# Two attention layers in one kernel: the linear layer's token forms prepared during the other layer, with another order of pairs

## The chip, the cores and the metric

The kernel runs on one core of a Trainium2 chip. TensorE (PE) multiplies matrices into eight accumulation banks. VectorE (DVE), ScalarE (ACT) and GpSimd (POOL) do the rest; POOL does not touch the banks here. SyncE (SP) issues all transfers from one queue, in order. The metric is the device time of one execution, in microseconds; less is better. The kernel before took 1781.55 us (median of three runs, 1781.36 to 1782.36).

## The reference

Two independent layers of 2048 tokens, width 1024 and 32 heads of 32 are computed and put side by side:

```python
# layer A: four segments of 512 tokens, causal softmax inside a segment,
# and a memory (M, z) that is read before and added to after each one
p = softmax(qs @ ks.T * scale + mask);  a_dot = p @ vs
a_mem = (phi(qs) @ M) / (phi(qs) @ z + 1e-6)
o = g * a_mem + (1 - g) * a_dot
M = M + phi(ks).T @ vs;  z = z + phi(ks).sum()

# layer B: linear attention with a learned feature map per head
q, k, v = split(x @ wqkv)
phi_q = concat(softmax(q @ w_phi), softmax(-q @ w_phi))     # and phi_k likewise
kv = phi_k.T @ v;  z = phi_k.sum()                          # over all 2048 tokens
o = (phi_q @ kv) / (phi_q @ z + 1e-6)
```

Each layer ends with a product by its output weights `wo`. Layer A is called attention here, layer B the linear layer.

## The kernel before, in words

**Precision.** Every large product is made of three 16-bit products. An fp32 operand is scaled, its upper half is copied to fp16 by ACT, and the rest is subtracted into a second fp16 half by DVE (`halves`, L388) or by POOL (`forms`, L466). The scale comes from the largest absolute value: a reduction per partition on DVE, a tiny product with a column of ones on PE that spreads it, and a few small operations on DVE.

**Strassen forms.** The linear layer works on pairs of 128-token blocks, eight pairs in all. A product of a pair (256 tokens by 1024) with a weight block is done as seven smaller products of combinations of blocks ("forms") in place of eight (`strassen`, L549 for the products, L555 and L559 for the sums of results on ACT and DVE). The seven forms of a pair take 7 x 256 KB. `xpair` makes them: it loads the raw tokens, finds the scale (L490 to L504), forms four sums on POOL (L458), splits the seven forms into halves (L388 or L466), and stores them in a scratch tensor `xf_d` (L526). `xkept` (L536) loads forms that were stored before, in two or three large transfers. The seven forms of a weight matrix are 1 MB each (`load_forms`, L475).

**Stages.** (1) Attention, up to about 930 us: 32 units, each a group of four heads in one segment; segments 0 and 1 first, then 2 and 3. Beside it the linear layer's query and key weights are multiplied with the feature map and turned into forms (`fold`). Segment 2 is loaded and split at unit 3 and segment 3 at unit 7 (`load_seg`), both needed only from unit 16 on. In the tail, pairs 6 and 7 get their forms, their values are computed and put away in `v_d`. (2) The key stage, to about 1265: for pairs 0 to 7 in this order a key product, the exponentials (L1112 to L1125), for pairs 0 to 5 the value product (splits at L1150 and L1152), and the sums kv (L1266). The next pair's forms are made meanwhile. `keep_bo` splits the linear layer's output weights here. (3) The query stage, to about 1600: queries, numerators, output product. (4) Attention's output product.

**What sets the order.** Every operation is recorded with an engine, a duration, a priority and its dependences, and a planner (`Graph.run`) writes the order of each engine from these: of the operations that are ready it takes the one with the lowest priority number. On the chip each engine then works through its list in that order and waits where an operand is late. `PB = 100` lies above all priorities of attention, so key-stage work fills attention's gaps. Buffers named `S0` to `S15` are slots of 8 KB per partition that pass from one stage to the next; a new owner waits for the readers of the one before.

Of the kernel before, what the change touches and what calls it, by code (L numbers as in the profile page):

```python
# [18 lines left out]
S = 2048  # L19
# [10 lines left out]
XS = (("S8", 4), ("S12", 3))  # L30
# [4 lines left out]
XL = (5, -0.2)  # L35
# [3 lines left out]
KS = (10, 14, 13, 4, 5, 6, 7)  # L39
XPLAN = ((None, 0, 0), (None, 1, 1), ((2, 3, "add"), 4, 3), ((0, 2, "subtract"), 2, 4), ((4, 0, "subtract"), 0, 2),  # L40
         ((1, 0, "subtract"), 1, 5), (None, 3, 6))
WPLAN = ((None, 0, 0), (None, 2, 1), (None, 3, 5), ((1, 0, "subtract"), 0, 3), ((3, 1, "subtract"), 1, 4),
# [201 lines left out]
def tile_kernel(ctx: ExitStack, tc: tile.TileContext, ax, aw, awv, awo, beta, bx, bwqk, bwv, bphi, bwo, out):  # L244
# [41 lines left out]
    wm = const.tile([128, 2], F32, name="wm")  # L286
    nc.gpsimd.memset(wm, 1.0)
# [8 lines left out]
    big = const.tile([128, 2], F32, name="big")  # L296
# [5 lines left out]
    bdm = ca.tile([128, NG, 132], F32, name="bdm")  # L302
# [181 lines left out]

    def xpair(p, raws, slots, prio, kind="pv", mode=DVE):
# [3 lines left out]
        for i, (rb, rv) in enumerate(raws):  # L489
# [4 lines left out]
        op(DVE, 0.1, lambda: nc.vector.tensor_reduce(top()[:, 0:1], top(), axis=AX.X, op=OP.max), w=[top], prio=prio)  # L494
        ps = bank(kind, [128, 2], "xscale")
        op(PE, 0.14, lambda: nc.tensor.matmul(ps(), top()[:, 0:1].to_broadcast([128, 128]), wm, start=True, stop=True),
           r=[top, wmb], w=[ps], prio=prio, short=True)
        op(DVE, 0.1, lambda: nc.vector.tensor_scalar(pst[:, p, 0:2], ps(), 2.0 ** -13, 1e-24, op0=OP.mult, op1=OP.max),
           r=[ps], w=[(pstb, (p, 0))], prio=prio)
        op(DVE, 0.12, lambda: nc.vector.reciprocal(pst[:, p, 2:4], pst[:, p, 0:2]), r=[(pstb, (p, 0))], w=[(pstb, (p, 1))], prio=prio)  # L500
        op(DVE, 0.1, lambda: nc.vector.scalar_tensor_tensor(
# [27 lines left out]
        return view_  # L529

    def xkept(p, slots, prio):

        t, view_, _ = xforms(slots)
        i = 0
# [1038 lines left out]
```

## Time and profile before

| | |
|---|---|
| median of three runs | 1781.55 us |
| profiled execution: first to last instruction | 1779.5 us |
| PE busy | 1715.4 us (96%) |
| DVE busy | 1457.1 us (82%) |
| ACT busy | 1130.8 us (64%) |
| POOL busy | 922.3 us (52%) |
| DMA, share of 16 engines | 44.9% |
| mean granted PE clock | 0.992 |

The busy time of PE counts overlapping products once. A wait is put down to the instruction that ended last before it; where an instruction waits for several, it can have been another. In a row of a group stand line, engine, operation, the names of the result and the operands, sizes and count, then busy us and mean ns of one, then the idle time just before. The names of the lines in the rows are those of the kernel before.

### The profile page before, as it was taken

How to read it: one execution, taken by the hardware profiler on the slowest of the kernel's cores; microseconds unless marked ns; L12 is line 12 of the kernel's file. 1: busy time of each engine (PE TensorE's matmuls, PEld its weight loads, DVE VectorE, ACT ScalarE, POOL GpSimd, SP SyncE). 2: the span in 40 equal slices, each digit the busy share in tenths (PEclk: the TensorE clock that was granted, in tenths of full speed). 3: DMA queues.
4: the chain of work that ended last, by engine and by line, in shares of the span. 5: the costliest groups of instructions: out<-in, count | busy, mean ns of one | idle time of the engine just before them, and what ended most of it. 6: DMA issues, size and time to landing. Idle time of an engine off the chain costs nothing. (4 is left out here: it accounts for less than half of the span.)

```text
span 1779.5 us, 38925 instructions
## 1 busy us (share of the span) xinstructions
PE 1715.4 (96%) x14712; PEld 1040.4 (58%) x14712; DVE 1457.1 (82%) x3367; ACT 1130.8 (64%) x2095; POOL 922.3 (52%) x1141
## 2 busy tenths in 40 slices
PE   7999999999999999999989989999899999999999
PEld 5767766677776777677644444444555444554444
DVE  6989989899787888788877999988997888877541
ACT  6897886987866878689674756444644454344441
POOL 6445454555756687777583544433456677431000
PEclk9999999999999999999989999999999999999999
DMA  6546555574545453674565244276411333133311
GB/s 208 169 144 183 159 153 158 167 225 129 160 128 156 109 179 110 161 217 121 179 202 193 96 168 137 113 272 227 139 49 63 119 125 107 66 143 137 119 65 65
DMA packets 173260, 258.92 MB, mean 146 GB/s; under 512 B 69904, under 2 KB 122896, under 8 KB 164368
## 3 DMA queue, kind: packets, MB, share of 16 engines
q1 hardware_dynamic: 173072, 256.44, 44.9%
q8 instruction: 115, 1.88, 0.4%
q14 instruction: 73, 0.60, 0.1%
HBM read 145.44 MB, written 85.00 MB: 129 GB/s over the span
## 5 line engine op out<-in xcount | busy, mean ns | idle before, releaser
L359 PE MATMUL proj<-S,S 128*128 128x128 f16 (+1 forms) x3072 | 502.7, 299 | 5.5 <-ACT S L386 3.6
L359 PEld LDWEIGHTS <-S 128*128 128x128 f16 x4608 | 331.3, 99 | 153.6 <-issue 8.9
L549 PE MATMUL proj<-S,S 128*128 128x512 f16 x1488 | 348.7, 382 | 12.3 <-ACT cs L555 3.9
L549 PEld LDWEIGHTS <-S 128*128 128x128 f16 x1968 | 189.0, 99 | 231.3 <-issue 17.2
L880 POOL TENSOR_SCALAR_AFFINE_SELECT ph<-ph 128x256 f16<-128x256 f16 (+1 forms) x448 | 196.3, 460 | 171.8 <-DVE ph L874 134.9
L874 DVE SCALAR_TENSOR_TENSOR ph<-s,ph 128x512 f16<-128x512 f32 x320 | 210.4, 683 | 56.5 <-ACT ph L873 54.5
L775 DVE CUSTOM_DVE_ANT_0 s<-s,causal 128x512 f32<-128x512 f32 (+3 forms) x512 | 242.3, 510 | 12.0 <-PE s L769 8.4
L871 ACT ACTIVATE s<-s,bd 128x512 f32<-128x512 f32 x320 | 212.2, 710 | 21.8 <-PE s L867 21.4
L873 ACT ACTIVATE ph<-s 128x512 f16<-128x512 f32 x320 | 190.4, 656 | 0.6
L1119 ACT ACTIVATE e<-e,sk 128x256 f32<-128x256 f32 x256 | 113.9, 497 | 98.3 <-DVE e L1116 94.5
L359 PE MATMUL misc<-S,ot 128*128 128x512 f16 x768 | 174.1, 379 | 0.0
L1415 POOL TENSOR_TENSOR e<-e,zb 128x512 f32<-128x512 f32 x64 | 84.5, 1343 | 71.5 <-DVE r L1122 65.8
L359 PEld LDWEIGHTS <-ot 128*128 128x128 f16 x768 | 73.4, 98 | 82.1
L769 PE MATMUL s<-S 96*128 96x512 f16 (+3 forms) x512 | 113.3, 300 | 5.8 <-DVE mt L775 4.2
L867 PE MATMUL s<-S 104*128 104x512 f16 (+3 forms) x512 | 113.9, 300 | 1.5 <-DVE quad L1011 0.8
L359 PE MATMUL proj<-wv,S 128*128 128x128 f16 x1536 | 104.2, 221 | 0.3 <-DVE mt L775 0.3
L903 PEld LDWEIGHTS <-ph 128*128 128x128 f16 x2560 | 87.8, 96 | 18.0 <-POOL ph L880 2.0
L1226 POOL TENSOR_TENSOR e<-e,r 128x1024 f32<-128x1024 f32 x32 | 64.4, 2017 | 61.3 <-DVE r L1125 50.4
L903 PE MATMUL pv<-vl,ph 128*128 128x66 f16 (+1 forms) x2560 | 92.9, 185 | 2.2 <-POOL ph L880 1.6
L1122 DVE TENSOR_REDUCE r<-e 128x32 f32<-128x1024 f32 x64 | 76.7, 1205 | 21.6 <-ACT e L1119 21.6
L1428 POOL TENSOR_TENSOR e<-e,r 128x1024 f32<-128x1024 f32 x32 | 62.9, 1970 | 41.9 <-DVE r L1426 38.3
L549 PE MATMUL s<-S,S 128*128 128x512 f16 x324 | 77.1, 379 | 1.8 <-ACT cs L555 1.8
(302 smaller groups left out, 3334.8 us busy)
## 6 DMA issues: line engine op xcount, KB each, us to landing
S<-h SPq DMA_DIRECT2D x192, 128.0 KB
S<-wf_d SPq DMA_DIRECT2D x21, 1024.0 KB
st<-bwqk SPq DMA_DIRECT2D x64, 256.0 KB
wf_d<-fo SPq DMA_DIRECT2D x48, 256.0 KB
out<-os SPq DMA_DIRECT2D x40, 256.0 KB
wf_d<-oT SPq DMA_DIRECT2D x36, 256.0 KB
S<-xf_d SPq DMA_DIRECT2D x9, 1024.0 KB
S<-aw SPq DMA_DIRECT2D x16, 512.0 KB
```

Source lines behind the costliest of these rows:

```text
L359: op(PE, dur, lambda c=c, a=a, b=b, lv=lv, rv=rv: nc.tensor.matmul(pv(), lv(), rv(), start=(c == 0 and a + b == 0), stop=(c == n - 1 and a ...
L549: op(PE, 0.215, lambda n=n, a=a, b=b, lv=lv, rv=rv: nc.tensor.matmul(ps(), lv(), rv(), start=(start and n == 0 and a + b == 0), stop=(n == ...
L769: nc.tensor.matmul(ps()[:, o:o + 128 * i + 128], st()[0:96, 0, h, 128 * i:128 * i + 128], st()[0:96, 1, h, 0:128 * i + 128], start=True, s ...
L775: dve(0.12 + 0.00113 * n, lambda h=h, i=i, o=o, n=n: nc.vector.tensor_tensor_reduce(ps()[:, o:o + n], ps()[:, o:o + n], causal[:, 512 - n: ...
L867: nc.tensor.matmul(ps()[:, o:o + n], st()[0:104, 1, h, 128 * j:128 * j + 128], st()[0:104, 0, h, 128 * j:512], start=True, stop=True)
L871: act(0.59, lambda: nc.scalar.activation(ps(), ps(), AF.Exp, bias=0.0, scale=bd()[:, 4, i2, 0:1]), r=[(bd, i2)], w=[ps])
L873: act(0.5, lambda: nc.scalar.activation(ph()[:, 0], ps(), AF.Copy, scale=2.0 ** 14), r=[ps], w=[(ph, 0)])
L874: dve(0.6, lambda: nc.vector.scalar_tensor_tensor(ph()[:, 1], ps(), 2.0 ** 14, ph()[:, 0], op0=OP.mult, op1=OP.subtract), r=[ps, (ph, 0)], ...
L880: nc.gpsimd.affine_select(pd, pd, pattern=[[0, n], [1, 128]], compare_op=OP.is_ge, fill=0.0, base=0, channel_multiplier=-1)
L903: nc.tensor.matmul(ps()[:, i, n0:n1], ph()[:, a, o:o + 128], vl()[:, j, h, n0:n1], start=(i == 0 and a == 0), stop=(j == min(i, 2)), skip_ ...
L1119: op(ACT, 0.41, lambda i=i: nc.scalar.activation(e()[:, 4 * i:4 * i + 4], e()[:, 4 * i:4 * i + 4], AF.Exp, bias=0.0, scale=sk()[:, i:i + 1 ...
L1415: op(POOL, 1.35, lambda a=a, h0=h0, e=e: nc.gpsimd.tensor_tensor(e()[:, 8 * a:8 * a + 8], e()[:, 8 * a:8 * a + 8], zv()[:, h0:h0 + 8], op= ...
```

## The change

1. **Preparation in attention.** A new function `prepare` makes the forms of pairs 6, 7, 0, 1 and 2 beside units 4, 6, 8, 15 and 27 of attention, in slots that are free there. DVE does the two maxima, ACT scales the raw blocks and makes the upper halves, POOL makes the four sums and all seven lower halves. Each form goes to `xf_d` by its own transfer. Pairs 3, 4 and 5 are prepared by the same function at the first three steps of the key stage, in `zb` and `kls`.
2. **Segments 2 and 3** are loaded at units 10 and 11 in place of 3 and 7, since the slots they use hold raw tokens first.
3. **Scales.** Token scales (`token_scale`) are found per pair, those of the values (`value_scales`) together, at unit 28 for five pairs.
4. **Tail.** The values of pairs 6, 7 and 0 are computed there, from forms that are loaded; pair 0's stay in the two `h3` buffers.
5. **Key stage.** The order of pairs is 0, 1, 6, 2, 3, 4, 7, 5; the last pair's values come before its keys. All pairs share one pair of buffers, and `xkept` reloads each of the seven forms alone as soon as its last reader is done. `keep_bo` is moved to steps 3 and 4 and its splits go to ACT and POOL. The seven query weight forms are loaded at the last step, where before six of them were loaded from the seventh step on.
6. **Query stage.** The second pair's forms have buffers of their own; the reloads are single there too.
7. Smaller: the masked memory update is two DVE operations with a small mask; halves of the value weights pass through new buffers `fp` and `fq`; other slots for the key weights.

```diff
-XS = (("S8", 4), ("S12", 3))
+XS = (("S10", 4), ("S14", 3))
+XB = (("S8", 4), ("S12", 3))
+SEQ = (0, 1, 6, 2, 3, 4, 7, 5)
+VFIRST = (7,)
+WQAT = 7
-KS = (10, 14, 13, 4, 5, 6, 7)
+KS = (8, 12, 13, 4, 5, 6, 7)
+PREP = {4: (6, 4), 6: (7, 5), 8: (0, 6), 15: (1, 11), 27: (2, 11)}
+SEGS = {10: 2, 11: 3}
+LATE = {0: 3, 1: 4, 2: 5}
+KEEPBO = {3: 0, 4: 1}
...
     def xkept(p, slots, prio):
-        t, view_, _ = xforms(slots)
-        i = 0
-        for b, (_, n) in zip(t, slots):
-            op(SP, 0.6, lambda b=b, i=i, n=n: nc.sync.dma_start(b(), xf_d[p, :, i:i + n]),
...
+        if slots is not XS:
+            t, view_, where = xforms(slots)
+        else:
+            t, view_, where = resident.get(0) or resident.setdefault(0, xforms(slots))
+        for f in XORDER:
+            b, i = where[f]
+            op(SP, 0.6, lambda b=b, i=i, f=f: nc.sync.dma_start(b()[:, i], xf_d[p, :, f]),
+               r=[(xfb, (p, f))], w=[(b, (f, a)) for a in range(2)], prio=prio, lat=1.0, kb=256)
         return view_
...
+    def prepare(p, prio, slot=None, dep=()):
+        late = slot is None
+        t = G.buf("b", [128, 2, 2, 512], F32, "zb") if late else G.buf("slot", [128, 2, 2, 512], F32, f"S{slot}")
+        top = G.buf("stage", [128, 2], F32, "xt", 2)
+        for i in range(2):
+            op(SP, 0.6, lambda i=i: nc.sync.dma_start(t()[:, i].rearrange("p a b -> p (a b)"), bx[2 * p + i].rearrange("p c n -> p (c n)")),
+               r=dep, w=[(t, (i, 0)), (t, (i, 1))], prio=prio, lat=1.0, kb=512)
+            op(DVE, 1.2, lambda i=i: nc.vector.tensor_reduce(
+                top()[:, i:i + 1], t()[:, i], axis=AX.XY, op=OP.max, apply_absolute_value=True),
...
+        token_scale(p, top, prio, "misc")
+        for i in range(2):
+            op(ACT, 1.05, lambda i=i: nc.scalar.activation(t()[:, i], t()[:, i], AF.Copy, scale=pst[:, p, 3:4]),
...
+        for n, (comb, k, f) in enumerate(XSELF):
...
+                op(POOL, 1.28, lambda i=i, j=j, k=k, o=o: nc.gpsimd.tensor_tensor(v(k), v(i), v(j), op=o),
...
+            op(ACT, 0.53, lambda h=h, k=k: nc.scalar.activation(h()[:, 0], v(k), AF.Copy), r=[key], w=[hk[0]], prio=prio)
+            e, ns, d = (DVE, nc.vector, 0.7) if n in LOWV else (POOL, nc.gpsimd, 1.28)
+            op(e, d, lambda h=h, k=k, ns=ns: ns.tensor_tensor(h()[:, 1], v(k), h()[:, 0], op=OP.subtract),
...
-        if u in (3, 7):
-            load_seg(2 + u // 4, 2 * u + 2.5, DVE)
+        if u in SEGS:
+            load_seg(SEGS[u], 2 * u + 2.5, DVE)
...
+        if u in PREP:
+            prepare(PREP[u][0], 2 * u + 4.5, PREP[u][1], [(un[u]["h3"], (1, 1))])
...
-    for n, p in enumerate(VT):
-        raw = G.buf("a", [128, 2, NC, 128], F32, "wv", 1)
...
+    for n, p in enumerate(VT + (0,)):
+        x = xkept(p, XB if n == 1 else XS, L - XL[n])
...
-    for p in range(NT // 2):
-        P = PB + 2 * p
-        if p in (1, 2):
-            keep_bo(p - 1, P + 0.5)
+    for at_, p in enumerate(SEQ):
+        P = PB + 2 * at_
+        if at_ in LATE:
+            prepare(LATE[at_], P + 0.5)
+            value_scales(LATE[at_], 1, LATE[at_], P + 0.5, "pv")
+        if at_ in KEEPBO:
+            keep_bo(KEEPBO[at_], P + 0.5)
...
+        if at_ in VFIRST:
+            strassen(x, wvf, P - 0.3, KB, CS, vout(p, vs, P - 0.3))
+            strassen(x, wkf, P, KB, CS, kout)
+        if at_ == WQAT:
+            wqf = load_forms(0, VS, P + 0.1, [])
+        if at_ < 7:
+            xn = xkept(SEQ[at_ + 1], XS, P - 0.5)
```

The order that results, at three places. First DVE in unit 8 of attention, before; `s,mt` are the row maxima of the scores, which the unit's later products wait for, and `xsc` marks the split of an input segment:

```order
L775 ISA s,mt<-s,causal 128x128
L775 ISA mt 128x1
L775 ISA s,mt<-s,causal 128x256
L775 ISA mt 128x1
L388 SCALAR_TENSOR_TENSOR S_4783<-S_4668,xsc,S_4783 128x512 x4
L775 ISA s,mt<-s,causal 128x256
L775 ISA mt 128x1
L775 ISA s,mt<-s,causal 128x512
```

The same four splits (second half of segment 3) now, in unit 13; L961 is the division of a finished unit:

```order
L807 ISA s,mt<-s,causal 128x128
L807 ISA mt 128x1
L807 ISA s,mt<-s,causal 128x512
L807 ISA mt 128x1
L961 TENSOR_TENSOR osum<-oall,rd 128x4x4x32
L398 SCALAR_TENSOR_TENSOR S_7266<-S_7166,xsc,S_7266 128x512 x4
L822 SCALAR_TENSOR_TENSOR mh<-mh,mt 128x4x4
```

The burst moved five units on and is still four long. Second, DVE in the key stage before; `mx`, `e` and `r` belong to the exponentials, `kls<-zb` are output weights and `S<-h` the next pair's forms:

```order
L1116 TENSOR_TENSOR e<-mx,cs 128x16x32
L388 SCALAR_TENSOR_TENSOR kls<-zb,wsc,kls 128x512 x4
L1114 TENSOR_TENSOR e<-cs,mx 128x16x32
L1116 TENSOR_TENSOR e<-mx,cs 128x16x32
L1112 TENSOR_REDUCE mx<-proj 128x16 x2
L1122 TENSOR_REDUCE r<-e 128x32
L1114 TENSOR_TENSOR e<-proj,mx 128x16x32
L1124 TENSOR_SCALAR r<-r 128x32
L1116 TENSOR_TENSOR e<-mx,proj 128x16x32
L388 SCALAR_TENSOR_TENSOR S_17059<-h_16716,pst,S_17059 128x512 x2
L388 SCALAR_TENSOR_TENSOR S_17059<-st,pst,S_17059 128x512
L1125 RECIPROCAL r<-r 128x32
```

And now, at the key stage's third step, where pair 5 is prepared (`xt<-zb`):

```order
L587 TENSOR_TENSOR cs<-cs,misc 128x512
L1094 TENSOR_REDUCE xt<-zb 128x1
L1343 TENSOR_TENSOR pt<-e,pt 128x512 x2
L1094 TENSOR_REDUCE xt<-zb 128x1
L1359 SCALAR_TENSOR_TENSOR kva<-kv,pst,kva 128x256
L1359 SCALAR_TENSOR_TENSOR za<-kv,za 128x4
L497 TENSOR_REDUCE tops<-xt 128x1
L1194 TENSOR_TENSOR e<-cs,mx 128x16x32
L1196 TENSOR_TENSOR e<-mx,cs 128x16x32
```

Of a pair's preparation only the two maxima and small operations are left on DVE. Third, SP's queue towards the end of the key stage, before; `wf_d` are the query weights, `xf_d` the forms of pairs:

```order
L1236 DMA ot<-v_d 128x1056 x4
L475 DMA S_18350<-wf_d 128x4096
L475 DMA S_18373<-wf_d 128x4096
L475 DMA S_18407<-wf_d 128x4096
L536 DMA S_18423<-xf_d 128x4096
L475 DMA S_18459<-wf_d 128x4096
L475 DMA S_18496<-wf_d 128x4096
L536 DMA S_18515<-xf_d 128x3072
```

And now, in the last step; `S_14072` is the shared buffer of forms and `S_18958` the second pair's:

```order
L485 DMA S_18824<-wf_d 128x4096
L485 DMA S_18851<-wf_d 128x4096
L1293 DMA bo_d<-kls 128x4096
L1271 DMA zb<-bwo 128x4x512
L485 DMA S_18937<-wf_d 128x4096
L565 DMA S_14072<-xf_d 128x1024
L485 DMA S_18951<-wf_d 128x4096
L565 DMA S_18958<-xf_d 128x1024 x4
L565 DMA S_14072<-xf_d 128x1024
```

The weights now stand between single reloads, each of which waits for PE to be done with the form that it replaces.

More of the change, by code (lines that the diff above doesn't have):

```diff
@@ L34 @@
 VLAG = 0.6
-XL = (5, -0.2)
+XL = (5, 4, 0.2)
 VPRIO = 0.9
@@ L1227, in kout @@
             es[i, hb] = e
[L1229 to L1231 removed]
+        if at_ not in VFIRST:
+            strassen(x, wkf, P, KB if p else ("proj",) * 3, CS, kout)
         for i in range(2):
```

164 lines of the change are left out of this document (100 added, 64 removed).

## The prediction

> **What bounds the kernel now.** I read the page's first part, then busy time by stretch, then the waits of TensorE (PE) stretch by stretch, then the granted clock, then the groups of VectorE (DVE) and GpSimd (POOL) where PE waits.
>
> ```profile
> span 1779.5 us, 38925 instructions
> PE 1715.4 (96%) x14712; PEld 1040.4 (58%) x14712; DVE 1457.1 (82%) x3367; ACT 1130.8 (64%) x2095; POOL 922.3 (52%) x1141
> ```
>
> PE is busy for all but 64 us. No matrix product is added or removed, so the change can only move those 64 us and what comes with them. By stretch (us busy of PE, PEld, DVE, ACT, POOL; then PE's granted clock, the DMA share and GB/s):
>
> ```profile
> 400.00:860.00 460.00, 458.60 (x5032) 325.82 (x5031) 379.16 (x1120) 348.17 (x637) 318.26 (x477) 1.00 0.51 148
> 860.00:930.00 70.00, 62.04 (x572) 36.62 (x571) 56.10 (x144) 52.01 (x93) 51.67 (x72) 0.94 0.60 193
> 1265.00:1600.00 335.00, 327.88 (x2242) 170.27 (x2240) 284.78 (x496) 160.48 (x319) 200.39 (x144) 1.00 0.29 98
> ...
> 200.00:330.00 130.00, 124.87 (x1323) 87.67 (x1322) 113.81 (x319) 107.17 (x194) 61.06 (x106) 0.97 0.47 144
> 330.00:490.00 160.00, 156.56 (x1740) 112.15 (x1738) 139.85 (x399) 128.84 (x237) 94.49 (x157) 1.00 0.60 180
> 490.00:560.00 70.00, 70.00 (x791) 51.24 (x789) 58.33 (x181) 49.03 (x92) 40.86 (x62) 1.00 0.45 132
> 930.00:1265.00 335.00, 310.79 (x2056) 154.06 (x2055) 303.56 (x505) 182.15 (x373) 140.78 (x109) 0.99 0.47 172
> 1000.00:1100.00 100.00, 92.51 (x627) 45.96 (x626) 98.38 (x173) 61.70 (x125) 43.98 (x37) 1.00 0.40 139
> ```
>
> The reader sees where the idle time lies: 24.2 us in the key stage (930 to 1265, where DVE is busy 91%), 8.0 in the tail of attention (860 to 930), 5.1 in 200 to 330, 3.4 in 330 to 490, 1.4 in 400 to 860, 7.1 in the query stage. Where DVE is near 82% PE hardly waits; where it is at 98% PE loses 7.5%. Who ended the waits (total us, times, longest), for 250 to 400, 860 to 930, 930 to 1240, 1240 to 1265 and 1265 to 1600:
>
> ```profile
> PE s L769 <- DVE mt L775: 4.0, 8, 0.9
> ...
> PE proj L549 <- ACT S L465: 3.3, 1, 3.3
> PE misc L496 <- DVE xt L494: 2.0, 1, 2.0
> PE pv L903 <- POOL ph L880: 1.6, 4, 0.9
> ...
> PE kv L1266 <- DVE ot L1152: 7.3, 6, 2.6
> PE proj L549 <- ACT cs L555: 3.3, 4, 1.4
> PE proj L549 <- DVE cs L559: 2.7, 2, 1.6
> ...
> PE kv L1266 <- DMA S<-xf_d: 3.9, 1, 3.9
> ...
> PE s L1434 <- POOL e L1428: 6.1, 7, 1.5
> ```
>
> A wait costs more than its idle time. First, the clock: in these stretches the granted clock (third number from the end) was 0.50, each right after a group of waits.
>
> ```profile
> 296.90:303.70 6.80, 5.93 (x47) 4.94 (x47) 6.73 (x31) 2.30 (x4) 0.00 (x0) 0.50 0.31 93
> 914.70:918.10 3.40, 3.28 (x10) 1.32 (x11) 0.38 (x1) 1.85 (x5) 3.21 (x5) 0.50 0.76 192
> 924.90:931.70 6.80, 5.83 (x36) 2.61 (x34) 3.18 (x6) 3.37 (x7) 4.47 (x5) 0.50 0.87 329
> 1259.50:1266.20 6.70, 6.13 (x48) 4.53 (x49) 5.88 (x12) 4.50 (x11) 3.92 (x4) 0.50 0.08 32
> ```
>
> Half of each length is lost: 3.4, 1.7, 3.4 and 3.4 us. Second, products are pipelined: five take 1.24 us where one takes 0.38, so they follow each other at 0.215, and each wait also uncovers some 0.16 us.
>
> ```profile
> 892.88 1.24 PE L549 MATMUL proj<-S,S 128*128 128x512 f16 x5
> ```
>
> The half clock at 296.9 began after waits of 0.9 us and less, so here a group of short ones sufficed. [...]
>
> **The change, part by part.** *Token forms of pairs 1 to 5 leave the key stage's DVE.* In 930 to 1265 the lines L388 (splitting forms and output weights) and L491 (the maxima) took, as busy time of DVE, the first two rows; the third is POOL with L458, the sums for these forms:
>
> ```profile
> 930.00:1265.00 335.00, 53.88 (x56) 0.99 0.47 172
> ...
> 930.00:1265.00 335.00, 12.11 (x10) 0.99 0.47 172
> ...
> 930.00:1265.00 335.00, 30.02 (x21) 0.99 0.47 172
> ...
> L1116 DVE TENSOR_TENSOR e<-mx,cs 128x512 f32<-128x512 f32 x26 | 23.7, 911 | 0.0
> L1116 DVE TENSOR_TENSOR e<-mx,proj 128x512 f32<-128x512 f32 x8 | 5.4, 675 | 0.0
> L1152 DVE SCALAR_TENSOR_TENSOR ot<-cs,pst,ot 128x512 f16<-128x512 f32 x18 | 16.1, 916 | 1.7 <-ACT ot L1150 1.6
> L559 DVE TENSOR_TENSOR cs<-cs,proj 128x512 f32<-128x512 f32 x17 | 11.4, 672 | 2.5 <-PE proj L549 2.5
> L1259 POOL TENSOR_TENSOR pt<-e,pt 128x512 f16<-128x512 f32 x32 | 40.7, 1277 | 65.4 <-ACT pt L1256 65.4
> ```
>
> Off DVE: 53.9 + 12.1 = 66.0. Pair 0's values, now made in the tail, take 3 adds of 0.67 and 4 splits of 0.92 = 5.7 more. Back come the maxima of pairs 3, 4 and 5, which are still prepared here: 6 x 1.21 = 7.3. DVE goes from 303.6 to about 239. PE loses pair 0's 84 value products, 84 x 0.215 = 18.1, to the tail: 310.8 becomes 292.7. DVE is then at 82% of PE's work instead of 91% of the stretch. The rows at that share are 400 to 860 (0.3% idle) and 1265 to 1600 (DVE 85%, 2.1%): 293 us would idle 0.9 to 6.2. I take 6, from the stage with the same products. The end of the stage I leave as it is, with about 5 and its half clock: the last product still has to go through subtraction, exponential, sum, POOL and copies before its last sums. So 24.2 becomes 11: **-13.2**; bounds -20 and 0.
>
> What hides the rest: POOL loses 30.0 and gains (3 x 11 + 16) x 1.28 = 62.7, so 141 becomes 173 of some 310 us. ACT was busy 182 of 335 and swaps splits for copies of like number. If that cover goes, every wait on POOL's pt and e grows by up to one operation, 1.28.
>
> *Attention, 200 to 330.* The splitting of input segment 3, which stood at unit 8, goes to units 12 and 13; pairs 7 and 0 are prepared instead. One segment on DVE, and what PE did beside it:
>
> ```profile
> L388 DVE SCALAR_TENSOR_TENSOR S<-S,xsc,S 128x512 f16<-128x512 f32 x8 | 5.8, 783 | 0.0
> L422 DVE TENSOR_REDUCE twb<-S 128x4 f32<-128x2048 f32 x2 | 4.5, 2275 | 0.0
> ...
> 290.69 2.74 DVE L388 SCALAR_TENSOR_TENSOR S<-S,xsc,S 128x512 f16<-128x512 f32 x4
> ...
> 293.89 0.38 PE L769 MATMUL s<-S 96*128 96x384 f16 x2 [0.81 <-DVE mt L775]
> 297.04 0.58 PE L769 MATMUL s<-S 96*128 96x512 f16 x1 [0.53 <-DVE mt L775]
> ```
>
> A segment is 10.3 us of DVE, in bursts that hold up the maxima; two preparations are 4 x 1.21 = 4.8 and some small operations. DVE falls from 113.8 to about 109 of 130 (84%). At 83% (490 to 560) PE did not wait. Bounds of the idle time 0 and 5.1; I take 1.5, nearer to the like row: -3.6, and the half clock at 296.9 goes, -3.4. **-7.0.**
>
> *Attention, 330 to 490.* Here both segments arrive: 139.9 + 2 x 10.3 + 2.4 (pair 1's maxima) = 163 us of DVE work in 160; some of it can slide to 490 to 560, where DVE has 12 us free. Bounds of PE's idle time: 3.4 as now, and 7.5% of 160 = 12 by the 98% row. I take 8, between them, since part slides: **+4.6**. POOL's 14 us per preparation (11 x 1.28) meets 61 of 130 and 94 of 160 busy; 318 of 460 harmed nothing.
>
> *Tail.* The scale of a pair is now found earlier and its forms come by DMA, so the 3.3 (forms from ACT) and the 2.0 (scale from DVE) go; the 1.6 on POOL's masks stays. The half clock at 914.7 followed the 3.3. Pair 0's values add 18.1 us of PE work that needs little else, a filler for a stretch that waits. **-5.3 - 1.7 = -7.0**; bounds -13 and +4, the second if a reload now arrives as late as the 3.9 blamed on DMA above.
>
> *Single reloads, order of pairs, weights.* 126 loads of 256 KB stand for 21 larger ones, some 14 MB more over 850 to 1600 where DMA is busy 0.29 to 0.60: hidden, unless SP's order hurts (below). A form is reloaded as soon as its last product is done; next it is needed six products later, 6 x 12 x 0.215 = 15.5 us. The query weights move the other way: they can only follow the values of the last pair, in front of its keys, with 7 x 12 x 0.215 = 18 us or more to land. The splitting of the memory update in two is 24 short operations over 800 us of DVE that is 18% free: 0.
>
> *Fewer waits*, about a dozen at 0.16: **-2.0**.
>
> Sum: -13.2 - 7.0 + 4.6 - 7.0 - 2.0 = -24.6. The profiled span of 1779.5 becomes 1754.9. The median of the runs is 1781.55, 2.05 above the span; with that kept: **1757 us**.
>
> **The rivals.**
> *SP's one queue (slower, 1790).* Reloads now wait in SP one by one for PE.
>
> ```profile
> SPq L536 <- PE proj L549: 83.0, 16, 12.2
> ```
>
> Sixteen waits of 5.2 us; what stands behind them in the queue, in the query stage the stores of the one output buffer that ACT and then PE need back, waits too. There are 49 reloads in that stage after the first pair. If each passes 0.7 us on to PE, 34 us go and the gain with them: that is the point from which it decides. Against it: in 1265 to 1600 no wait of weight ended on SP or DMA, only on POOL.
> *GpSimd takes the room back (1770).* The key stage gains 49 POOL operations and loses 21. DVE operations that read two buffers outside the banks ran 911 ns where the same from a bank ran 675. If each of the 28 more held DVE for its whole length, 28 x 1.28 = 36, DVE would be at 275 of 293 (94%) and the 13.2 would not be won. [...] Against full blocking: 26 operations lost 0.24 each, not 1.28.
> *DVE full in 330 to 490 (1776).* If nothing slides: 12 idle, 3 of overflow and two or three half-clock stretches (8), 19 worse than my +4.6.
> *Query weights late (1767).* 7 MB at the stretch's 172 GB/s take 41 us where 18 to 40 are covered; some 10 us. For it: the 3.9 above. Against: the ACT copy that those sums need began at 1258.5, after POOL, so that wait was hardly the DMA's.
>
> ```profile
> 1258.47 1.67 ACT L1256 ACTIVATE pt<-e 128x512 f16<-128x512 f32 x3 [4.37 <-POOL e L1226]
> ```
>
> *All waits of the key stage go (1742).* The 11 us left there and the half clock at 1259.5.
>
> **How the numbers follow.** Forecast 0.40, SP queue 0.16, GpSimd 0.14, DVE full 0.12, all waits 0.10, weights late 0.08. All but the SP queue are faster; I give a part of the 1776 case to no change, taking 0.2% (3.6 us) as what a measurement of this kernel can tell from none: faster 0.78, same 0.05, slower 0.17. The range takes in every case but the slower one: 1738 to 1786; the forecast's own, from its bounds, is 1745 to 1767.
>
> **What would show it.** Key stage: DVE near 82%, PE idle near 11, no scale matmul or form wait in the tail; in 200 to 330 no half clock; in 330 to 490 DVE near 100% with PE idle near 8. Wrong if PE's waits in the query stage end on reloads or output stores, if DVE's two-buffer operations run well over 1 us, or if new half-clock stretches appear in attention.

## The result, and the profile after

The changed kernel took **1766.43 us** (median; 1763.92 to 1768.99) beside 1781.95 for the kernel before: a ratio of 0.9900 (95% interval 0.9887 to 0.9913), 15.5 us faster. Forecast were 1757 us, 24.6 us faster. The profiled executions stand 13.3 us apart (1779.5 and 1766.2).

The head of the page, then busy time by stretch of the changed kernel (columns as in the prediction: PE, PEld, DVE, ACT, POOL, granted clock, DMA share, GB/s):

```profile
span 1766.2 us, 39229 instructions
PE 1714.1 (97%) x14722; PEld 1040.3 (59%) x14722; DVE 1430.7 (81%) x3330; ACT 1147.8 (65%) x2115; POOL 978.2 (55%) x1191
```

```profile
200.00:330.00 130.00, 122.12 (x1292) 85.53 (x1291) 113.72 (x316) 116.76 (x209) 87.61 (x129) 0.97 0.57 176
330.00:490.00 160.00, 156.31 (x1695) 110.65 (x1694) 151.56 (x411) 127.15 (x230) 91.55 (x145) 1.00 0.66 206
860.00:930.00 70.00, 67.14 (x613) 40.73 (x612) 50.60 (x145) 44.60 (x80) 31.29 (x57) 0.98 0.60 179
930.00:1265.00 335.00, 319.27 (x2123) 159.37 (x2122) 282.46 (x460) 194.57 (x397) 180.65 (x136) 0.98 0.56 193
1265.00:1600.00 335.00, 328.59 (x2246) 170.84 (x2245) 285.14 (x497) 155.60 (x303) 193.17 (x142) 0.99 0.30 96
```

The last sum kv, which ends the key stage's own work, now ends at 1255.3, before at 1271.4; so some 10 us of the row 930 to 1265 already belong to the query stage (VectorE was busy 273.4 us up to 1255.3). PE's idle time fell in the tail (8.0 to 2.9) and in the key stage (24.2 to 15.7), and rose at 200 to 330 (5.1 to 7.9), where ScalarE is now the fullest engine beside PE: 116.8 of 130 us. Half clock costs 17 us, 14 before: three of its stretches (1044.6, 1099.2, 1147.0; 13.7 us together) lie in the key stage, where before there was one of 6.7 at its end. Two of them, each with the 3.4 us ahead of it, in which PE was busy for only 0.72 and 0.34 us:

```profile
1040.95:1044.36 3.41, 0.72 (x4) 0.36 (x4) 3.41 (x6) 3.36 (x9) 0.00 (x0) 1.00 0.00 0
1044.57:1047.98 3.41, 3.41 (x10) 1.24 (x9) 3.41 (x8) 3.41 (x10) 1.28 (x1) 0.50 0.52 154
1095.70:1099.10 3.40, 0.34 (x2) 0.06 (x1) 1.63 (x2) 2.46 (x6) 0.35 (x1) 1.00 0.23 86
1099.20:1106.00 6.80, 5.76 (x32) 2.69 (x32) 6.62 (x11) 1.19 (x3) 3.16 (x3) 0.50 0.00 0
```

Who ended PE's waits, at 930 to 1250 (three rows; L583 and L587 were L555 and L559, L1350 was L1266) and at 200 to 330 (two; L909 makes the lower halves of the probabilities and was L874):

```profile
PE proj L577 <- ACT cs L583: 5.3, 3, 2.8
PE proj L577 <- DVE cs L587: 4.4, 2, 4.2
PE kv L1350 <- DVE pt L1343: 4.2, 6, 1.6
...
PE s L902 <- DVE ph L909: 3.0, 3, 1.5
PE s L801 <- DVE ph L909: 1.5, 1, 1.5
```

The groups of VectorE in the key stage show why it is still late there. The same kind of operation takes 676 ns when one operand lies in a bank (`proj`), and 940 to 1237 ns when both are buffers (692 with nothing beside it, run 8 below); the first fence is the changed kernel, the second gives two of these groups of the kernel before that were not shown yet:

```profile
L1343 DVE TENSOR_TENSOR pt<-e,pt 128x512 f16<-128x512 f32 x31 | 31.4, 1030 | 0.8 <-ACT pt L1340 0.8
L1196 DVE TENSOR_TENSOR e<-mx,cs 128x512 f32<-128x512 f32 x25 | 30.9, 1237 | 0.0
L1194 DVE TENSOR_TENSOR e<-cs,mx 128x512 f32<-128x512 f32 x25 | 23.5, 940 | 0.0
L1232 DVE SCALAR_TENSOR_TENSOR ot<-cs,pst,ot 128x512 f16<-128x512 f32 x15 | 20.2, 1357 | 0.0
L1196 DVE TENSOR_TENSOR e<-mx,proj 128x512 f32<-128x512 f32 x8 | 5.4, 676 | 0.0
```

```profile
L1259 DVE TENSOR_TENSOR pt<-e,pt 128x512 f16<-128x512 f32 x31 | 22.9, 756 | 1.4 <-ACT pt L1256 1.3
L1114 DVE TENSOR_TENSOR e<-cs,mx 128x512 f32<-128x512 f32 x26 | 19.8, 761 | 0.0
```

One of the waits, followed back by the timelines of VectorE, GpSimd and PE: two splits take 3.92 us and a subtraction 2.40 while GpSimd runs its multiplications; PE then waits 4.21 us and the half clock at 1099.2 follows.

```profile
1088.80 3.92 DVE L1232 SCALAR_TENSOR_TENSOR ot<-cs,pst,ot 128x512 f16<-128x512 f32 x2
1092.64 2.40 DVE L1194 TENSOR_TENSOR e<-cs,mx 128x512 f32<-128x512 f32 x1
...
1089.81 4.68 POOL L1308 TENSOR_TENSOR e<-e,r 128x1024 f32<-128x1024 f32 x2
...
1100.24 2.29 PE L577 MATMUL proj<-S,S 128*128 128x512 f16 x5 [4.21 <-DVE cs L587]
```

### The profile page after: what moved, and what is told of

Same layout as the page of the kernel before. It is cut to its first block, busy times and chain, and to the rows that moved or that the text cites. A ratio compares the mean times of both kernels' runs of the same rounds, so it can differ in the third digit from the quotient of the medians.

```text
span 1766.2 us, 39229 instructions
## 1 busy us (share of the span) xinstructions
PE 1714.1 (97%) x14722; PEld 1040.3 (59%) x14722; DVE 1430.7 (81%) x3330; ACT 1147.8 (65%) x2115; POOL 978.2 (55%) x1191
## 4 chain that ended last, share of the span: by engine, by line
PE 52%; DVE 17%; ACT 4%; issue 1%; DMA 1%; POOL 0%; ACTq 0%; DVEq 0%; POOLq 0%
PE proj L369 12%; PE proj L577 11%; PE misc L369 8%; PE proj L1590 5%; PE s L1590 2%; DVE mx L1192 2%; PE s L902 2%; DVE e L1196 2%; PE s L801 2%; PE pv L938 2%; DVE r L1202 2%; DVE e L1194 1%; ACT e L1199 1%; PE misc L1590 1%; PE pv L1536 1%
## 5 line engine op out<-in xcount | busy, mean ns | idle before, releaser
L577 PE MATMUL proj<-S,S 128*128 128x512 f16 x1584 | 368.8, 384 | 11.3 <-DVE cs L587 5.9
L909 DVE SCALAR_TENSOR_TENSOR ph<-s,ph 128x512 f16<-128x512 f32 x320 | 210.1, 683 | 55.6 <-ACT ph L908 53.1
L906 ACT ACTIVATE s<-s,bd 128x512 f32<-128x512 f32 x320 | 212.7, 713 | 23.5 <-PE s L902 21.1
L807 DVE DVE_READ_ACCUMULATOR2_ANT mt<- 128x1 f32 x512 | 72.3, 141 | 0.0
```

The costliest lines, as they stand in the source:

```text
L577: op(PE, 0.215, lambda n=n, a=a, b=b, lv=lv, rv=rv: nc.tensor.matmul(ps(), lv(), rv(), start=(start and n == 0 and a + b == 0), stop=(n == ...
L807: dve(0.12 + 0.00113 * n, lambda h=h, i=i, o=o, n=n: nc.vector.tensor_tensor_reduce(ps()[:, o:o + n], ps()[:, o:o + n], causal[:, 512 - n: ...
L906: act(0.59, lambda: nc.scalar.activation(ps(), ps(), AF.Exp, bias=0.0, scale=bd()[:, 4, i2, 0:1]), r=[(bd, i2)], w=[ps])
L909: dve(0.6, lambda: nc.vector.scalar_tensor_tensor(ph()[:, 1], ps(), 2.0 ** 14, ph()[:, 0], op0=OP.mult, op1=OP.subtract), r=[ps, (ph, 0)], ...
```

## The experiments

Every run but the eighth is the changed kernel with the edit shown (runs 1, 5 and 12 also take the value scales of the moved pairs at unit 28). The table gives its median and ratio to the kernel before with the 95% interval; the kernel before took 1782.0 to 1784.0 us beside them, so differences of a microsecond or two between rows are read from the ratios. Then, from the profile, come PE's idle us in four stretches and, last, the us lost to half clock (half of the stretches at 0.50, without the first 17 us and the end of the program). Where a kernel is longer ahead of a stretch, that stretch holds other work by as much. Each edit also makes the planner write another order from its place on, so a run never changes one wait alone, and what the runs cost does not add up part by part.

| kernel | us | ratio | 200-330 | 330-490 | 490-860 | 930-1265 | clock |
|---|---|---|---|---|---|---|---|
| before | 1782 | 1 | 5.1 | 3.4 | 1.0 | 24.2 | 13.7 |
| changed | 1766.4 | 0.9900 (0.9887-0.9913) | 7.9 | 3.7 | 0.5 | 15.7 | 17.1 |
| 1 all pairs in attention | 1796.3 | 1.0067 (1.0053-1.0081) | 7.2 | 3.9 | 14.6 | 8.5 | 32.4 |
| 2 pairs 7, 0 later | 1786.7 | 1.0016 (1.0004-1.0029) | 1.6 | 6.3 | 8.8 | 12.2 | 27.3 |
| 3 output weights on DVE | 1771.7 | 0.9928 (0.9916-0.9941) | 8.0 | 3.6 | 0.4 | 20.1 | 18.8 |
| 4 last pair's keys first | 1779.7 | 0.9974 (0.9961-0.9988) | 7.9 | 3.6 | 0.5 | 21.9 | 17.1 |
| 5 all, in own slots | 1772.0 | 0.9933 (0.9920-0.9946) | 7.9 | 3.8 | 12.1 | 9.4 | 11.9 |
| 6 units shifted by one | 1783.3 | 1.0003 (0.9995-1.0012) | 6.0 | 8.7 | 3.3 | 16.5 | 17.1 |
| 7 reloads in two pieces | 1777.2 | 0.9964 (0.9951-0.9978) | 7.8 | 4.0 | 0.7 | 31.8 | 22.2 |
| 9 first half undone | 1786.3 | 1.0022 (1.0011-1.0032) | 2.6 | 1.3 | 11.2 | 16.2 | 29.0 |
| 10 pairs 0 to 7 | 1773.3 | 0.9951 (0.9939-0.9964) | 7.2 | 4.0 | 0.8 | 23.3 | 20.5 |
| 11 upper halves on DVE | 1772.3 | 0.9943 (0.9931-0.9956) | 3.7 | 6.5 | 4.7 | 15.9 | 18.8 |
| 12 two more in attention | 1770.4 | 0.9925 (0.9909-0.9942) | 7.2 | 3.9 | 3.1 | 16.8 | 25.6 |

### GpSimd beside VectorE

**8. The engines by themselves.** Loops of VectorE's forms, alone and beside GpSimd, then PE's products in groups with waits.

> Only small loops, none of the layers' work; the output is zeros. First VectorE's forms (two buffers, split, one operand in a bank, row maxima, a small operation of 16 columns) alone and then beside a row of GpSimd's lower halves or sums. Contention theory: operations with two buffer operands go from about 0.68 us to 1.3 or more on average beside GpSimd, and a small one can take over 1 us; those with one operand in a bank and the maxima stay within 5%. Rival (a share of bandwidth, the same for all): all forms slow by 10 to 40% alike. Then PE's products in groups with waits between: (10 products, one ScalarE copy), (40, one), (40, two), (40, four), (40, eight). [...]

Groups by stretch: the two-buffer operation alone, then the 15 that ran while GpSimd made lower halves; the split in the same way; one operand in a bank beside GpSimd; the small operation alone and beside it; and GpSimd itself, beside the row maxima and with the first 15:

```profile
L99 DVE TENSOR_TENSOR dw<-da,db 128x512 f32<-128x512 f32 x24 | 16.6, 692 | 0.8
L99 DVE TENSOR_TENSOR dw<-da,db 128x512 f32<-128x512 f32 x15 | 22.9, 1524 | 0.5
L102 DVE SCALAR_TENSOR_TENSOR dc<-da,sc,dc 128x512 f16<-128x512 f32 x24 | 18.0, 752 | 0.8
L102 DVE SCALAR_TENSOR_TENSOR dc<-da,sc,dc 128x512 f16<-128x512 f32 x15 | 22.8, 1523 | 0.5
L105 DVE TENSOR_TENSOR dw<-dw,ps 128x512 f32<-128x512 f32 x24 | 16.5, 687 | 0.8
L111 DVE TENSOR_TENSOR sm<-sm 128x16 f32<-128x16 f32 x48 | 8.4, 175 | 1.6
L111 DVE TENSOR_TENSOR sm<-sm 128x16 f32<-128x16 f32 x48 | 21.1, 439 | 1.6
...
L114 POOL TENSOR_TENSOR ph<-pa,ph 128x512 f16<-128x512 f32 x16 | 18.4, 1152 | 1.2
L114 POOL TENSOR_TENSOR ph<-pa,ph 128x512 f16<-128x512 f32 x15 | 22.3, 1485 | 1.2
```

The contention theory holds: of the forms tried, only those with two buffer operands suffer. A whole-size one that meets a lower half of GpSimd takes 0.83 us longer (1524 ns for 692), and GpSimd's operation 0.33 (1485 for 1152). The small operation's mean rises from 175 to 439 ns: the 48 take 12.7 us longer (21.1 for 8.4), which is 0.79 for each of GpSimd's 16 lower halves. So the price of a lower half is much the same for both sizes, and in proportion the small one pays most. The maxima (686 ns over all 72, alone and beside GpSimd) and a bank operand (687 in the same way) do not suffer. The two engines do not simply take turns: GpSimd's lower halves repeat every (22.3 + 1.2) / 15 = 1.57 us with a VectorE operation each, where 1.15 + 0.69 would be 1.84. What the products did is told at the end.

**1 and 5. All pairs prepared in attention.** In run 1 pairs 3, 4 and 5 share S11 with the value weights, in run 5 pairs 2 to 5 have S0 to S3.

```diff
-PREP = {4: (6, 4), 6: (7, 5), 8: (0, 6), 15: (1, 11), 27: (2, 11)}
-LATE = {0: 3, 1: 4, 2: 5}
+PREP = {4: (6, 4), 6: (7, 5), 8: (0, 6), 15: (1, 11), 18: (3, 11), 21: (4, 11), 24: (5, 11), 27: (2, 11)}  # run 1
+PREP = {4: (6, 4), 6: (7, 5), 8: (0, 6), 15: (1, 11), 17: (2, 0), 20: (3, 1), 23: (4, 2), 26: (5, 3)}  # run 5
+LATE = {}
```

> Pairs 3, 4 and 5 are prepared in attention too (units 18, 21 and 24), so the key stage loses 33 sums and lower halves of GpSimd (about 42 us at 1.28), six maxima of VectorE (7.3 us) and their copies on ScalarE. Contention theory: the operations of VectorE that read two buffers outside the banks (L1196 e<-mx,cs, mean 1237 ns in the changed kernel's key stage, 911 before) fall below 1050 ns, VectorE's busy time in the key stage falls by about 25 us, PE's idle time there from 15.7 to about 9 and its half-clock time from 13.6 us to 7 or less: 1757 to 1760 us in all. Rival (the waits come from the stage's own chain of subtraction, exponential, sum and copies): the mean falls but the idle time stays within 3 us of 15.7, and three more preparations beside attention cost up to 5 us as the first two did: 1765 to 1771 us.

> As the first run (all pairs prepared in attention), but pairs 2 to 5 get raw slots of their own (S0 to S3, free once segments 0 and 1 are read) at units 17, 20, 23 and 26, in place of sharing S11 with the value weights. Theory that attention lost 30 us there because ScalarE, in order, stood behind preparations that waited for the shared raw slot and for GpSimd: PE's idle time at 560 to 860 us falls from 14.5 back towards 3, half-clock stretches there from five to at most one, the key stage keeps its gain (idle 4 in place of 15): 1755 to 1762 us. Rival (it is the preparations' work as such, 14 us of GpSimd and 7 of ScalarE beside each unit, that delays phi): attention still loses 20 to 30 us: 1780 to 1796 us.

In the key stage the theory was right twice. VectorE falls by 23 us in run 1 (the row below against 282.46), of which 7.3 are maxima (the stage of run 1 lies 30 to 45 us later; from the first sum kv to the last the fall is 26.6); PE's idle time falls by about 7, and in run 5 no half clock is left there. (The one group picked in the expectation did not fall below 1050 ns: L1196 took 1091 in run 1 and 1242 in run 5, where L1343 fell to 819 and L1194 to 804.) In attention run 1 lost all of it and 30 us more. Rows of run 1: the key stage, 560 to 860, and two rows from just ahead of its half clock at 667: an operation of VectorE that took 1.94 us where 0.69 is usual, beside GpSimd's lower half of a weight form, and a copy of ScalarE that stood 1.28 us behind the store of the buffer it fills:

```profile
930.00:1265.00 335.00, 326.46 (x2208) 161.89 (x2208) 259.69 (x462) 187.58 (x386) 140.01 (x123) 0.99 0.55 183
560.00:860.00 300.00, 285.48 (x3017) 201.46 (x3015) 237.58 (x681) 225.46 (x405) 250.72 (x336) 0.95 0.59 172
...
662.47 1.94 DVE L961 TENSOR_TENSOR osum<-oall,rd 128x512 f32<-128x512 f32 x1
666.97 0.63 ACT L475 ACTIVATE fp<-S 128x512 f16<-128x512 f32 x1 [1.28 <-DMA wf_d<-fp]
```

Own slots took back most of that, but not to 3: 12.1 us of idle time and 10.2 us at half clock stay at 490 to 860. At 1772.0 run 5 lies between its two forecasts.

**3. The output weights' splits back on VectorE.**

```diff
...
-                op(ACT, 0.53, lambda raw=raw, t=t, i=i: nc.scalar.activation(t()[:, 0, i], raw()[:, i], AF.Copy),
...
-                op(POOL, 1.28, lambda raw=raw, t=t, i=i: nc.gpsimd.tensor_tensor(t()[:, 1, i], raw()[:, i], t()[:, 0, i], op=OP.subtract),
...
+                halves(*((t, (a, i), lambda a=a, t=t, i=i: t()[:, a, i]) for a in range(2)), (raw, i, lambda raw=raw, i=i: raw()[:, i]),
+                       (wscs, (1, n), lambda: wsc[:, 1, n]), 512, prio)
```

> The splits of the output weights go back to VectorE (16 operations of 0.8 to 0.95 us, some 14 us) and away from GpSimd (16 lower halves of 1.35 us, 21.6 us) and ScalarE (8 scalings). Contention theory: each operation of GpSimd that goes gives VectorE back 0.7 to 1 us, so VectorE's busy time in the key stage stays within 5 us and the time within 2 us of 1766: no gain from having moved them. Rival (GpSimd is free cover and VectorE's own load decides): VectorE gains the full 14 us, PE's idle time grows by 5 to 8: 1771 to 1775 us.

1771.7, nearer to the rival. At 1000 to 1265 VectorE was busy 240.2 us (233.7 in the changed kernel) and GpSimd 131.9 (152.1): the 16 splits themselves took 16.3 us there (14 were expected), so 9.7 came back from other operations, 0.61 per operation of GpSimd that went. So contention pays back more than half, and the move to GpSimd was worth some 5 us all the same.

**12. Two more pairs in attention.**

```diff
+PREP = {4: (6, 4), 6: (7, 5), 8: (0, 6), 15: (1, 11), 20: (3, 0), 23: (4, 1), 27: (2, 11)}
+LATE = {2: 5}
```

> Pairs 3 and 4 are prepared beside units 20 and 23 in the free slots S0 and S1, pair 5 alone stays in the key stage (third step), pair 2 stays at unit 27 in S11. GpSimd loses 22 long operations in the key stage. Contention theory, from the run with all pairs in own slots (first kv sum to last 271.3 us against 287.3): two thirds of those 16 us, 8 to 11, are won there; 600 to 800 us loses 3 to 6 as in that run and the loss at 830 us (unit 26) does not come: 1759 to 1763 us, faster than the changed kernel. Rival (queue order): a new stall with a half clock somewhere between 560 and 930 us takes it back, 1766 to 1774 us.

1766.6 to 1776.6, median 1770.4: no better than the changed kernel. The profiled execution is its slowest; its key stage:

```profile
930.00:1265.00 335.00, 318.25 (x2140) 159.21 (x2138) 264.20 (x441) 183.90 (x378) 153.53 (x116) 0.98 0.53 183
```

600 to 860 lost little (2.7 us of idle time), but the key stage gained little: VectorE there falls by 18 us, to 264.2, yet PE's idle time stays (16.8) and so does the half clock, and first sum kv to last takes 283.4 us against 287.3, not 8 to 11 less. The new half clock that the rival expected stands in the tail, at 910.3 (6.8 us). So less contention alone does not settle what PE waits for; in run 5, with 11 operations of GpSimd fewer still, the waits did fall.

### Where preparation stands in attention

**2. Pairs 7 and 0 later.**

```diff
+PREP = {4: (6, 4), 15: (1, 11), 18: (7, 11), 21: (0, 11), 27: (2, 11)}
```

> The preparations of pairs 7 and 0 move from units 6 and 8 (where segment 3 was split before) to units 18 and 21; nothing else is changed. Theory that they filled ScalarE at 200 to 330 us (117 of 130 us busy, and the chain of phi ended the waits): PE's idle time in that stretch falls from 7.9 to about 2, the half clock at 269.8 us (6.8 us long) goes, and the whole gains 6 to 9: 1758 to 1760 us. Rival (the waits come from the order of that unit's work, whoever fills the gaps): idle time stays above 5 there, or the same waits turn up at units 18 and 21: 1764 to 1768 us.

Each was right for a stretch and neither for the time: at 200 to 330 PE's idle time is 1.6 with no half clock, and the kernel is 20 us slower. New waits stand at 330 to 490, 560 to 860 and in the tail. One of them, on VectorE's timeline: the second of two operations on the row maxima's halves takes 1.24 us where 0.18 is usual (median of 32), and PE waits 1.7 for it.

```profile
379.34 1.24 DVE L822 SCALAR_TENSOR_TENSOR mh<-mh,mt 128x16 f16<-128x16 f16 x1
```

**6. Units shifted by one.**

```diff
+PREP = {5: (6, 4), 7: (7, 5), 9: (0, 6), 15: (1, 11), 27: (2, 11)}
```

> The first three preparations stand one unit later (units 5, 7 and 9 in place of 4, 6 and 8), nothing else. Work per stretch is the same within one unit. If the terms of a stretch (busy shares) set the waits, the time stays within 3 us of 1766. Rival (which operation happens to stand ahead of phi and of the maxima in the engines' queues decides): attention's waits move by 5 us or more in either direction, 1756 to 1780 us.

1783.3: the whole gain is gone, though the work of each stretch is the same. Rival right, and more: idle time rises from 3.7 to 8.7 at 330 to 490, and by 3 more at 490 to 860.

**9. The first half undone.**

```diff
+PREP = {17: (6, 0), 19: (7, 1), 21: (0, 2), 23: (1, 3), 26: (2, 11)}
+SEGS = {3: 2, 7: 3}
```

> The input segments 2 and 3 go back to units 3 and 7, and the preparations of pairs 6, 7, 0, 1 and 2 all move to units 17, 19, 21, 23 and 26, into slots S0 to S3 and S11; pairs 3, 4 and 5 stay in the key stage. Up to 490 us the work is then that of the kernel before. If busy shares set the waits as the prediction took it, 200 to 330 goes back to 5 us of idle time and a half clock at 297, 330 to 490 to 3.4, and the five preparations after 490 cost what their share of GpSimd and ScalarE gives (under 3): 1764 to 1768 us. Rival (queue order, and the small operations of VectorE that wait for GpSimd's long ones): the second half of attention loses 8 to 25 us as in the runs with three or four preparations there: 1775 to 1795 us.

1786.3, as the rival has it. The first half is not the same as before either: 200 to 490 is better (3.8 us idle against 8.6), 0 to 200 worse (15.5 against 11.2, two half clocks at 164 and 192); why was not followed.

**11. Upper halves on VectorE.**

```diff
-            op(ACT, 0.53, lambda h=h, k=k: nc.scalar.activation(h()[:, 0], v(k), AF.Copy), r=[key], w=[hk[0]], prio=prio)
+            op(DVE, 0.5, lambda h=h, k=k: nc.vector.tensor_copy(h()[:, 0], v(k)), r=[key], w=[hk[0]], prio=prio)  # in attention
```

> In the five preparations beside attention the seven upper halves are copied by VectorE, not by ScalarE; ScalarE keeps the two scalings. Theory that ScalarE's queue held up phi at 262 to 273 us: ScalarE falls from 117 to about 109 of 130 us at 200 to 330, PE's idle time there from 7.9 to 3 to 5, the half clock at 269.8 goes, VectorE gains 7 us: 1760 to 1764 us. Rival (VectorE ends those waits as well, since maxima, phi and splits are its own and its copies meet GpSimd's lower halves): idle time there stays at 6 or more and the stretch 330 to 490 loses 3 to 8: 1768 to 1776 us.

ScalarE is what held 200 to 330: with it at 111.2 us, PE's idle time there is 3.7 and the half clock at 269.8 is gone, although VectorE is now busy 125.6 of the 130 us. In the changed kernel, ScalarE's and VectorE's timelines show how: scaling and two copies of a preparation stand ahead of the probabilities, and VectorE waits 1.79 us.

```profile
268.63 1.37 ACT L1099 ACTIVATE S<-S,pst 128x1024 f32<-128x1024 f32 x1
269.67 0.85 ACT L1118 ACTIVATE fp<-S 128x512 f16<-128x512 f32 x1
270.19 0.85 ACT L1118 ACTIVATE fq<-S 128x512 f16<-128x512 f32 x1
...
271.56 0.69 DVE L909 SCALAR_TENSOR_TENSOR ph<-s,ph 128x512 f16<-128x512 f32 x1 [1.79 <-ACT ph L908]
```

But the rival's second half came too: at 381 the four splits of a segment, which do no harm in the changed kernel, hold up the maxima (VectorE, then PE, of run 11), and 13.7 us at half clock follow, the larger part after six more waits for GpSimd's masks, which come after VectorE (3.5 us together):

```profile
381.17 4.64 DVE L398 SCALAR_TENSOR_TENSOR S<-S,xsc,S 128x512 f16<-128x512 f32 x4
...
386.14 0.38 PE L902 MATMUL s<-S 104*128 104x384 f16 x2 [2.10 <-DVE mt L807]
```

### The end of the key stage

**4. The last pair's keys first**, **10. pairs 0 to 7**, **7. reloads in two pieces.**

```diff
-VFIRST = (7,)
+VFIRST = ()                          # runs 4 and 10
-SEQ = (0, 1, 6, 2, 3, 4, 7, 5)
-WQAT = 7
+SEQ = (0, 1, 2, 3, 4, 5, 6, 7)       # run 10
+WQAT = 6                             # run 10
...
-        for f in XORDER:
-            op(SP, 0.6, lambda b=b, i=i, f=f: nc.sync.dma_start(b()[:, i], xf_d[p, :, f]),
...
+        for b, (_, n) in zip(t, slots):
+            op(SP, 0.6, lambda b=b, i=i, n=n: nc.sync.dma_start(b(), xf_d[p, :, i:i + n]),   # run 7
...
```

> At the last step the key product comes before the value product, as at every other step; the query weights use the value weights' slots and can then be loaded only after the last value product. Theory that the order keys-last covers both the query weights and the last pair's exponentials: about 7 x 12 x 0.215 = 18 us of cover goes from the weights while the sums kv come no earlier, so PE waits 10 to 25 us at the start of the query stage: 1776 to 1792 us. Rival (the exponentials of the last pair are what ends the stage, and with the keys first they are covered by the values): the end of the key stage loses its waits (5 us, half clock) and the weights arrive in time: 1760 to 1766 us.

> Pairs run 0 to 7 again in the key stage, so the last two steps have no value product and the query weights are loaded from the seventh step on, as before; all else is as changed. Theory that the order of pairs and the last pair's values in front of its keys are worth the end of the stage: the waits at 1200 to 1265 come back (9.3 us of stalls at 1250 to 1300 and a half clock at 1259 before), and the middle of the stage gets denser for VectorE: 1771 to 1778 us. Rival (the order is worth nothing, since weights and last exponentials are covered either way): 1764 to 1768 us.

> Every reload of a pair's seven forms is two transfers of 1 MB and 768 KB again, not seven of 256 KB; the shared buffers stay. Theory that single reloads were hidden and so were larger ones: a piece is free three or four products (7.7 or 10.3 us) before it is needed again and 1 MB at 196 GB/s takes 5.4 us; the time stays within 2 us of 1766. Rival A (the single reloads gave part of the gain): PE waits for forms up to 2 us at seven pairs in each of two stages: 1775 to 1795 us. Rival B (SP's one queue is filled by them): fewer transfers, 1758 to 1764 us.

1779.7 (+13), 1773.3 (+7) and 1777.2 (+11). The times of the first two came as their theories had it. Run 7 (its profiled execution is the slowest of nine) has the size of rival A but not its place: PE waited 0.2 us for a form, once, and lost its time at the end of the key stage (31.8 us idle at 930 to 1265). There PE has nothing to do when the last exponentials stand behind the last products. The waits of PE at 1100 to 1260 in run 10, then in run 7:

```profile
PE kv L1350 <- ACT pt L1340: 7.4, 1, 7.4
PE s L577 <- ACT cs L583: 4.8, 1, 4.8
```

```profile
PE kv L1351 <- ACT pt L1341: 13.9, 2, 10.4
PE proj L578 <- ACT cs L584: 3.2, 1, 3.2
```

In the changed kernel the longest wait there, 4.2, is the one at 1100 shown above, and 1200 to 1255 has 3.3 us of idle time where run 10 has 15 (1200 to 1258). Run 4 is slower, but not by the weights as far as the profile shows: its last sum kv comes 5.5 us earlier (1249.6 against 1255.1), where the theory had it no earlier, and from there to the end it takes 13.5 us longer. PE idles 5.8 us in the first 60 of that, against 1.8, and none of these waits ends on a transfer. The larger part of the 13.5 us is work of PE, which had done less ahead of the sums. Why the order that the planner wrote for run 7 leaves nothing beside the last exponentials was not followed further.

## Why the prediction was right in sign and too large

The time lay inside the range and just inside the forecast's own 1745 to 1767, 9.4 us above 1757. Two of the signs that it named for being wrong came all the same: two-buffer operations of VectorE ran over 1 us (1030 to 1357 ns in three of four groups), and attention has a half clock at 269.8. By its steps:

- **Tail, -7.0: right, measured -8.5.** Idle 8.0 to 2.9, half clock 5.1 us to 1.7. The 3.3 on forms and the 2.0 on the scale are gone; what is left (2.8) waits for GpSimd's sum of outputs.
- **Key stage, -13.2: right in kind, mis-sized; measured -5.1.** Idle fell by 8.5, not 13.2, and half clock rose by 3.4 us, where it was taken to stay. The step that failed is "DVE goes from 303.6 to about 239". It went to 282.5, or to 273.4 up to the last sum. The rival *GpSimd takes the room back* bounded this at 36 us, with VectorE at 275; by the four groups above against their means before (911, 761, 916 and 756 ns) VectorE lost 25 x 0.33 + 25 x 0.18 + 15 x 0.44 + 31 x 0.27 = 28 us. I took zero for it in the forecast. Its argument against (0.24 us lost per operation before) was a mean at a lower load of GpSimd; run 8 gives 0.83 for an operation that meets one of GpSimd's. The conclusion of the rival, that nothing of the 13.2 is won, did not follow: VectorE was busy 84% of 930 to 1255.3, where the rival had 94%. But neither does 84% go with an idle time near 11, as the rows at that share had it: what PE waited for ahead of 1100 were single operations of up to 2.4 us in a chain, and a share does not show these.
- **200 to 330, -7.0: wrong, measured +2.8.** The step "Bounds of the idle time 0 and 5.1" costed two preparations as VectorE's 4.8 us; it looked at GpSimd's share and not at ScalarE's queue. They put 14 copies and four scalings on ScalarE, which is at the head of the chain for the probabilities. Run 11 and run 2 each take that away, and the idle time goes to 3.7 and 1.6.
- **330 to 490, +4.6: too dark, measured +0.3.** VectorE at 151.6 of 160 us (95%) cost nothing. The idle time came out at its lower bound, and busy share was no guide within the bounds: run 2 has 146.5 us of VectorE there and 6.3 idle, run 11 147.3 and 6.5. What decides in the timelines of these two is which operation stands ahead of the maxima or their halves when PE needs them.
- **Single reloads, order of pairs, query weights, 0: that they would not hurt was right; that they do nothing is not borne out.** Undone, the single reloads cost 11 us (run 7), the order of pairs with the last pair's order and the weights 7 (run 10), and the last pair's order alone 13 (run 4). The prediction gave them no part in the gain. That undoing more costs less than undoing one shows that these are prices of whole plans; what each part is worth alone stays open. *SP's one queue* and *query weights late* did not happen: no wait of PE ended on a reload or on weights, and fewer transfers (run 7) made the kernel slower.
- **Fewer waits, -2.0.** Idle time and half clock by stretch add up to about -9 (0 to 200 and the query stage each lost 1.7 to a half clock more); the spans differ by 13.3. PE's waits went from 73 to 51 in number, where the prediction had about a dozen fewer; at its 0.16 each that is 3.5 us of the 4 to 5 between, an estimate. The rest is not resolved.

That a like kernel with three preparations one unit later is 17 us slower (run 6) says how far the sum can be trusted. The same working would have given run 6 much the same 1757, and it came out level with the kernel before. So the sign rests on the stages that the prediction read rightly and, in part, on luck with the places in attention, whose terms were smaller than what the order of the queues moves.

## What to carry to other kernels

Work that is moved into another stage's gaps must be costed on every in-order queue it enters, above all the one whose short operations feed TensorE (ScalarE's at 200 to 330 here, where VectorE waited 1.79 us behind a scaling and two copies); a busy share says little about it (VectorE at 95% of 330 to 490 left PE 3.7 us idle, at 92% in run 2 6.3). When GpSimd takes over elementwise work, add something like half a microsecond of VectorE for each of its operations if VectorE works on two buffers at the time, an estimate from 0.61 in run 3 and 0.83 in run 8, where two really meet. After such a move, try a few neighbouring places: here they differed by more than the whole gain (17 us in run 6, where the gain is 15.5).

## What the runs showed of the hardware

**Half clock began on a grid of 3.41 us.** In the profiles of the kernel before and of the changed one the stretches at half clock begin whole multiples of 3.413 us apart (before at 20.39, 296.87, 914.68, 924.92 and 1259.43; changed at 17.19, 269.78, 904.66, 1044.60, 1099.22, 1147.00 and 1594.15). Cut by this grid from 30 us on to the last whole window, the two have 6 windows at full clock in which PE was busy under 1.5 us of the 3.41, and half clock followed each; with 1.5 to 2.2 us it followed in 4 of 18, with 2.2 to 2.6 in none of 14, over 2.6 in none of 965. Run 8 has two equal waits of 2.57 us between groups of 40 products: the first, held nearly whole by one window, was followed by half clock, the next, split between two windows, was not. Windows at 622.5 (the first wait, half clock next), and at 632.7 and 636.2 (the second, none):

```profile
622.50:625.90 3.40, 1.07 (x5) 0.48 (x5) 0.00 (x0) 2.18 (x4) 0.00 (x0) 1.00 0.00 0
625.90:629.30 3.40, 3.40 (x10) 1.20 (x9) 0.00 (x0) 0.00 (x0) 0.00 (x0) 0.50 0.00 0
...
632.70:636.20 3.50, 2.61 (x13) 1.07 (x11) 0.00 (x0) 0.83 (x2) 0.00 (x0) 1.00 0.00 0
636.20:639.60 3.40, 1.72 (x8) 0.78 (x8) 0.00 (x0) 1.56 (x3) 0.00 (x0) 1.00 0.00 0
```

In that run the granted clock stayed at 1.00 with a wait of 0.74 us after every ten products (408 to 456), and with 1.3 us after every forty (539 to 600). So the reading of the prediction, that a group of short waits suffices, was borne out only where they added up inside one window, as ahead of the prediction's 296.9, where PE was busy 1.51 us of the 3.41.

**The grid's place against the program differs from profile to profile.** Counted from the first instruction, its lines lie at 3.32 us in the kernel before, 0.12 in the changed one and 2.08 in run 10 (each and multiples of 3.413 after it). The changed kernel and run 10 have the same work and nearly the same waits at 212 to 217 us. In the first they fall into two windows, in the second into one, and 6.8 us at half clock follow; both 1.92 and 1.65 lie in the band in which half clock followed 4 times of 18 (rows of the changed kernel, then of run 10):

```profile
211.75:215.16 3.41, 1.92 (x11) 1.00 (x10) 0.72 (x2) 3.41 (x8) 1.39 (x2) 1.00 0.47 154
215.16:218.57 3.41, 3.16 (x52) 2.48 (x51) 3.38 (x17) 3.41 (x8) 3.30 (x6) 1.00 0.10 39
```

```profile
213.71:217.12 3.41, 1.65 (x12) 0.99 (x11) 1.61 (x5) 3.41 (x9) 1.25 (x3) 1.00 0.23 85
217.12:223.95 6.83, 6.83 (x77) 5.99 (x77) 5.70 (x26) 6.83 (x13) 6.30 (x10) 0.50 0.20 78
```

Half of these 6.8 us, 3.4, is what the two profiles differ by in a stretch that nothing was changed in; a term of that size needs medians, or the waits themselves.
